# Five scheduler streams instead of three in a fused linear-attention and SwiGLU kernel

## The chip, the cores and the metric

The kernel runs on one core of one Trainium2 chip. The metric is the device time of one execution in microseconds (us), lower is better. "Time" is the median of several executions; "span" is the time from the first to the last instruction in the one execution that was profiled, and is about 1.7 us shorter than the time of the same execution. PE is the matmul engine (TensorE), PEld its loading of weights, DVE the vector engine, ACT the scalar engine, POOL the GpSimd engine, SP the engine that issues loads and stores.

## The reference, cut to what matters

`x` has 2048 rows of 640 numbers (16 tiles of 128 rows). The block is `x + A(norm(x)) + B(norm(x))`, where both branches read the same layer norm:

```python
xn = layernorm(x)
# A: attention with a learned feature map, 32 heads of 20
q, k, v = split(xn @ wqkv)
phi(u)  = concat(softmax(u @ w_phi), softmax(-u @ w_phi))      # per head
kv, z   = sum over all rows of phi(k)^T v,  sum of phi(k)      # needs every row
o       = phi(q) kv / (phi(q) . z)
A       = o @ wo
# B: SwiGLU
B       = (silu(xn @ w1) * (xn @ w3)) @ w2
```

Two facts of this shape matter. The sums over rows (`kv`, `z`) are a barrier: no output of attention can be made before the last key row has been normalised. The MLP (branch B) has no such barrier: each block of 512 rows needs only its own four normed tiles. The MLP is cut into 4 blocks of 12 chunks; a chunk is 10 matmuls of 128x512.

## The kernel before

A small scheduler in Python runs when the kernel is built. Streams (generators) yield steps; each step is a list of instructions with estimated costs. The scheduler always commits the step whose PE work could start first. Once committed, the order of instructions on each engine is fixed in the program, with a semaphore wait where an input comes from another engine. The timelines show the engines working through their lists in that order: in e2_coupled ACT stands 12.09 us for one instruction while a tanh that is ready stands behind it.

```python
def attention():                       # stream 1 of 3: (attention, mlps, outs)
    yield lambda: (loads(), consts())
    yield lambda: ln(0, 2); yield lambda: ln(2, 2)
    ... # fold w_phi into K's weights (fold_t, fold_mm), transpose x tiles 0-3
    for t in range(T):
        yield lambda t=t: kv_tile(t, banks("A", 4))     # K and V, exp, key normalise
        if t < 6:
            yield lambda t=t: ln(4 + 2 * t, 2)          # norms of two later tiles
        if t < 12:
            yield lambda t=t: xn_transpose(t + 4, banks("A", 1), "ACT" if t % 2 else "DVE")
        if t == 2:
            ... # fold_t for Q
            done["fold"] = True
    ... # q_proj(0), K/V sums; done["kv"] = True; then the query blocks

def ln(t0, n):      # DVE bn_stats, bn_aggr; POOL rstd = (var+eps)^-0.5; DVE (x-m)*rstd
    ...
def kv_tile(t, k):
    ... # 20 matmuls; ACT: exp(+), exp(-), copy of V; DVE: tensor_reduce, reciprocal
    ... # POOL: two multiplies of 128x640 ("key normalise")

def mlps():
    for b in range(NB):
        for fc in range(FC):
            while not done["fold"] or (b >= 2 and not done["kv"]):
                yield None                              # held
            yield lambda b=b, fc=fc: mlp(b, fc, banks("M", 2))
```

In the scheduler loop a step without PE work was committed at once (`at = -1.0`). `mlp` needs, for each chunk, one tanh on ACT and two products on DVE. `hT2`, the MLP's result for block 2, lay on the bytes of the keys (`ekt`), which is why block 2 was held until the K/V sums were done; `wqk_s` (weights of Q and K) lay on `hT1`.

The softmax here doesn't subtract the row's maximum and nothing guards it: scores larger than these inputs give would overflow.

Of the kernel before, what the change touches and what calls it, by code (L numbers as in the profile page):

```python
# [9 lines left out]
D = 640  # L10
# [18 lines left out]
class _Op:  # L29
    __slots__ = ("part", "eng", "emit", "reads", "writes", "cost", "dma", "deps", "start", "end",  # L30
                 "inc", "count", "sem", "clock", "idx")

    def __init__(self, eng, emit, reads, writes, cost, dma=False):
        self.eng, self.emit, self.reads, self.writes = eng, emit, reads, writes
        self.cost, self.dma = cost, dma
        self.part = False
        self.inc = False
        self.count = 0
        self.sem = None


class _Program:
# [52 lines left out]
    def op(self, eng, name, writes, reads, args, kw=None, cost=0.1):  # L95
# [4 lines left out]
        o = _Op(eng, lambda: m(*args, **kw), r, w, cost)  # L100
        o.part = eng == "POOL" and any(a.start_partition() != 0 for a in writes)
# [3 lines left out]
    def dma(self, eng, out, in_):  # L105
# [5 lines left out]
        o = _Op(eng, lambda: m(out, in_), self.regions(in_), self.regions(out), nbytes, True)  # L111
        self.pending.append(o)
# [36 lines left out]
    def ready(self, ops):  # L149
# [8 lines left out]
        return t  # L158

# [74 lines left out]
def bass_parallel_sum__linear_kernel_hedgehog__glu_gated_swiglu__prompt_kernel(  # L234
# [37 lines left out]
    bst = new("bst", [128, T, 2, 6], f32)  # L272
    mv = new("mv", [128, T, 2], f32)
    rstd = new("rstd", [128, T], f32)
# [14 lines left out]
    KVc = new("KVc", [128, 2, DC, D], bf, RX)  # L289
    ZG = new("ZG", [128, 2, DC, 64], bf, RX + 12800)  # L290
    wo_s = new("wo_s", [128, DC, D], bf, RX + 14080)
# [4 lines left out]
    EqT1 = new("EqT1", [128, 2, DC, 512], bf, RKV)  # L296
# [4 lines left out]
    wqk_s = new("wqk_s", [128, DC, 2 * D], bf, RH + 24576 - 12800)  # L301
# [3 lines left out]
    hT2 = new("hT2", [128, FC, 512], bf, RE)  # L305
    hT3 = new("hT3", [128, FC, 512], bf, RE + 12288)
    w2_s = new("w2_s", [128, FC, D], bf, RE + 24576)
# [8 lines left out]
    EqT0 = new("EqT0", [128, 2, DC, 512], bf, RW)  # L316
    EqT = [EqT0, EqT1]

    E_s = new("E_s", [128, 4, 128], f32, RW + 10240)
    den_s = new("den_s", [128, 4, 32], f32, RW + 12288)  # L320
# [47 lines left out]

    def memset(eng, o, v):
        P.op(eng, "memset", [o], [], (o, v), cost=0.15 + free(o) / 960)  # L370
# [14 lines left out]
    def loads():  # L385
        P.dma("SP", x_tok[:, 0:2, :], x_t[:, 0:2, :])
        P.dma("SP", x_tok[:, 2:4, :], x_t[:, 2:4, :])
        P.dma("SP", phi_s[:], phi_t)
        P.dma("SP", wqk_s[:, :, D:2 * D], wqkv_t[:, :, D:2 * D])
        P.dma("SP", wv[:], wqkv_t[:, :, 2 * D:3 * D])  # L390
        P.dma("SP", x_tok[:, 4:8, :], x_t[:, 4:8, :])
        P.dma("SP", x_tok[:, 8:12, :], x_t[:, 8:12, :])
        P.dma("SP", wqk_s[:, :, 0:D], wqkv_t[:, :, 0:D])
        for q in range(2):
            P.dma("SP", w1_s[:, :, 768 * q:768 * q + 768], w1_t[:, :, 768 * q:768 * q + 768])
            P.dma("SP", w3_s[:, :, 768 * q:768 * q + 768], w3_t[:, :, 768 * q:768 * q + 768])
            if q == 0:
                P.dma("SP", x_tok[:, 12:16, :], x_t[:, 12:16, :])
# [21 lines left out]
    def ln(t0, n):  # L420
        for t in range(t0, t0 + n):
            for q in range(2):
                i = x_tok[:, t, 320 * q:320 * q + 320]
                P.op("DVE", "bn_stats", [bst[:, t, q, :]], [i], (bst[:, t, q, :], i), cost=0.42)
            o, i = mv[:, t, :], bst[:, t, :, :].rearrange("p a b -> p (a b)")
            P.op("DVE", "bn_aggr", [o], [i], (o, i), cost=0.2)
        v, r = mv[:, t0:t0 + n, 1], rstd[:, t0:t0 + n]
        P.op("POOL", "tensor_scalar_add", [r], [v], (r, v, EPS), cost=0.3)
        tt("POOL", r, r, mhalf[:, 0:n], ALU.pow)
        for t in range(t0, t0 + n):  # L430
            o, m, s = x_tok[:, t, :], mv[:, t, 0:1], rstd[:, t:t + 1]
            P.op("DVE", "tensor_scalar", [o], [o, m, s], (o, o, m, s, ALU.subtract, ALU.mult),
                 cost=0.33)

    def xn_transpose(t, k, eng):
# [328 lines left out]
```

## Time and profile before

| | before |
|---|---|
| time, median of 3 runs | 354.18 us (353.96 to 354.21) |
| span | 352.9 us |
| PE busy | 313.8 us, 89% |
| first MLP matmul | 52.4 us |
| last K/V sum | 171.5 us |

The first two parts of the profile's page: the busy time of each engine, and tenths of busy time in 40 slices of 8.8 us.

```profile
PE 313.8 (89%) x2114; PEld 183.1 (52%) x2114; DVE 178.6 (51%) x299; ACT 117.7 (33%) x193; POOL 61.1 (17%) x68
PE   0582739968999999997999999999999999999996
PEclk9997878996999999999999999999999999999999
```

PE is the busiest engine, and its idle time is concentrated in the first nine slices. The clock that was granted to it is also lower there. The table of windows says how much (columns after the window's length: busy us of PE, PEld, DVE, ACT and POOL with the number of instructions, then granted clock, busy share of the DMA engines, GB/s):

```profile
0.00:18.00 18.00, 4.63 (x39) 3.99 (x39) 11.56 (x22) 5.77 (x9) 9.36 (x20) 1.00 0.92 302
18.00:80.00 62.00, 42.89 (x286) 26.11 (x286) 34.73 (x66) 24.69 (x38) 16.93 (x20) 0.88 0.17 59
80.00:172.00 92.00, 88.51 (x620) 53.78 (x621) 55.34 (x93) 40.42 (x64) 34.80 (x28) 0.97 0.03 10
172.00:350.00 178.00, 177.73 (x1170) 99.25 (x1170) 76.36 (x120) 46.78 (x82) 0.00 (x0) 1.00 0.13 41
```

After 172 us PE has almost no idle time. In the first 80 us it is busy 47.5 us, and no other engine is saturated either. So something makes them wait for one another. The timeline shows what (start, duration, engine, instruction, and in brackets idle time before it and whose end ended it):

```profile
26.43 1.49 DVE L100 TENSOR_REDUCE S_59<-ekt 128x64 f32<-128x1280 bf16 x1 [3.62 <-ACT ekt L100]
27.95 0.55 DVE L100 RECIPROCAL rS_60<-S_59 128x64 f32<-128x64 f32 x1
28.59 2.50 POOL L100 TENSOR_TENSOR ekt<-ekt,rS_60 128x640 bf16<-128x640 bf16 x2 [10.77 <-DVE rS_60 L100]
30.54 0.21 DVE L100 BATCH_NORM_AGGREGATE mv<-bst 128x2 f32<-128x12 f32 x1
31.05 0.22 POOL L100 TENSOR_SCALAR rstd<-mv 128x2 f32<-128x2 f32 x1
31.35 0.71 POOL L100 TENSOR_TENSOR rstd<-rstd,mhalf 128x2 f32<-128x2 f32 x1
32.09 0.80 DVE L100 TENSOR_SCALAR x_tok<-x_tok,mv,rstd 128x640 bf16<-128x640 bf16 x2 [1.34 <-POOL rstd L100]
32.60 0.72 PE L100 MATMUL PS<-ident,x_tok 128*128 128x128 bf16 x5 [6.18 <-DVE x_tok L100]
```

DVE sums the keys of one tile (reduce, reciprocal) and only then takes the statistics of the next x tiles; POOL normalises the keys (2.50 us) and only then computes `rstd` for those x tiles; DVE stands still for it, then applies the norm; PE has been idle for 6.18 us when the transpose of that tile may start. The chain of waits goes through this cycle five times before 80 us. (All lines of the kernel are L100 or L101, a helper; instructions are told apart by tile names.)

### The profile page before, as it was taken

Reading aid. Unit: us, or ns where it says so; the run is one execution under the profiler, and the core shown is the slowest. Engines: PE = TensorE matmul, PEld = TensorE weight load, DVE = VectorE, ACT = ScalarE, POOL = GpSimd, SP = SyncE. Lnnn points to the kernel's source line nnn. Section 1 sums busy time; section 2 is a strip of 40 time slices with the busy share of each in tenths; the row PEclk is TensorE's granted clock in tenths of the full one; section 3 lists DMA queues with packets and bytes.
Section 4 is the critical chain, followed back from the end, with each engine's and each line's share of the span. In section 5 each row is a group of like instructions: output and inputs, shape, how many; then the busy total and the mean of one; then the engine's idle time right before and its main releaser. Section 6 shows DMA issues by size and latency. Waiting matters only on the chain.

```text
span 352.9 us, 4956 instructions
## 1 busy us (share of the span) xinstructions
PE 313.8 (89%) x2114; PEld 183.1 (52%) x2114; DVE 178.6 (51%) x299; ACT 117.7 (33%) x193; POOL 61.1 (17%) x68
## 2 busy tenths in 40 slices
PE   0582739968999999997999999999999999999996
PEld 0461425534555555656744544544545577777774
DVE  4836563585886675632459349249289011111111
ACT  1440535532535435680352562472431300000000
POOL 2703330330323432494000000000000000000000
PEclk9997878996999999999999999999999999999999
DMA  7991000000000002000440000000000112222211
GB/s 233 368 371 54 0 0 3 0 1 2 1 0 2 0 2 93 2 1 2 126 154 0 2 0 2 0 2 1 0 3 0 39 37 76 74 76 74 76 56 37
DMA packets 14214, 17.38 MB, mean 49 GB/s; under 512 B 1392, under 2 KB 14192, under 8 KB 14192
## 3 DMA queue, kind: packets, MB, share of 16 engines
q1 hardware_dynamic: 14192, 17.07, 15.0%
q8 instruction: 16, 0.26, 0.3%
q14 instruction: 6, 0.05, 0.0%
HBM read 14.44 MB, written 2.62 MB: 48 GB/s over the span
## 4 chain that ended last, share of the span: by engine, by line
PE 77%; DVE 9%; POOL 9%; ACT 1%; issue 1%; DMA 1%; POOLq 0%
PE PS L100 77%; POOL ekt L100 5%; DVE S_59 L100 2%; DVE x_tok L100 2%; POOL rstd L100 2%; POOL KVc L100 2%; ACT ekt L100 1%; DVE bst L100 1%; DVE rS_60 L100 1%; DMA x_tok<-in_A_x_dram 1%; DVE BDc L100 1%; DVE t_66 L100 1%; DVE Wkp L100 0%; DVE xnT L100 0%; DVE mv L100 0%
## 5 line engine op out<-in xcount | busy, mean ns | idle before, releaser
L100 PE MATMUL PS<-xnT,w_s 128*128 128x512 bf16 x480 | 113.7, 388 | 4.2 <-DVE t_66 L100 4.2
L100 PEld LDWEIGHTS PS<-xnT,w_s 128*128 128x128 bf16 x480 | 45.8, 99 | 59.6 <-DVE t_66 L100 7.0
L100 POOL TENSOR_TENSOR ekt<-ekt,rS_60 128x640 bf16<-128x640 bf16 x32 | 39.9, 1269 | 92.5 <-DVE rS_60 L100 92.5
L100 DVE SCALAR_TENSOR_TENSOR t_66<-th,PS 128x512 bf16<-128x512 f32 x48 | 32.4, 675 | 32.2 <-ACT th L100 32.2
L100 ACT ACTIVATE th<-PS 128x512 f32<-128x512 f32 x48 | 28.7, 597 | 56.0 <-PE PS L100 55.8
L100 DVE TENSOR_TENSOR xres<-PS,xres 128x640 bf16<-128x640 f32 x16 | 13.2, 824 | 64.6 <-PE PS L100 64.6
L100 DVE TENSOR_REDUCE S_59<-ekt 128x64 f32<-128x1280 bf16 x16 | 23.7, 1484 | 25.5 <-ACT ekt L100 25.5
L100 ACT ACTIVATE ekt<-PS 128x640 bf16<-128x640 f32 x32 | 20.8, 701 | 34.7 <-PE PS L100 34.7
L100 PE MATMUL PS<-Wkp,xnT 128*128 128x320 bf16 x160 | 26.7, 319 | 1.8 <-ACT xnT L100 1.1
L100 PE MATMUL PS<-wv,xnT 128*128 128x320 bf16 x160 | 25.0, 305 | 0.0
L100 PE MATMUL PS<-wo_s,oT 128*128 128x320 bf16 x160 | 24.4, 300 | 0.0
L100 PE MATMUL PS<-xnT,Wqp 128*128 128x512 bf16 x100 | 22.3, 380 | 0.0
L100 PEld LDWEIGHTS PS<-Wkp,xnT 128*128 128x128 bf16 x160 | 16.1, 103 | 11.7 <-ACT xnT L100 1.3
L100 ACT ACTIVATE oT<-PS 128x512 bf16<-128x512 f32 x20 | 11.9, 597 | 24.4 <-PE PS L100 24.4
L100 PEld LDWEIGHTS PS<-wv,xnT 128*128 128x128 bf16 x160 | 16.0, 100 | 6.7
L100 PEld LDWEIGHTS PS<-wo_s,oT 128*128 128x128 bf16 x160 | 15.5, 98 | 6.4 <-issue 0.2
L100 PE MATMUL PS<-ident,wqk_s 128*128 128x128 bf16 x50 | 5.1, 283 | 14.4 <-DMA wqk_s<-in_A_wqkv_dram 8.7
L100 DVE BATCH_NORM_STATS2 bst<-x_tok 128x6 f32<-128x320 bf16 x32 | 15.0, 469 | 3.5 <-DMA x_tok<-in_A_x_dram 3.0
L100 PEld LDWEIGHTS PS<-xnT,Wqp 128*128 128x128 bf16 x100 | 9.5, 98 | 11.2 <-ACT ekt L100 0.4
L100 PE MATMUL PS<-ident,x_tok 128*128 128x128 bf16 x80 | 8.1, 248 | 7.5 <-DVE x_tok L100 7.5
L100 DVE TENSOR_SCALAR x_tok<-x_tok,mv,rstd 128x640 bf16<-128x640 bf16 x16 | 9.4, 627 | 10.3 <-POOL rstd L100 10.3
L100 PE MATMUL PS<-w_s,hT_76 128*128 128x320 bf16 x96 | 13.7, 299 | 0.0
(71 smaller groups left out, 347.7 us busy)
## 6 DMA issues: line engine op xcount, KB each, us to landing
w_s<-in_B_w_dram SPq DMA_DIRECT2D x4, 960.0 KB, 12.3
xres<-in_A_x_dram SPq DMA_DIRECT2D x16, 160.0 KB, 2.4
out_dram<-xres SPq DMA_DIRECT2D x16, 160.0 KB, 1.8
x_tok<-in_A_x_dram SPq DMA_DIRECT2D x3, 640.0 KB, 10.0
w_s<-in_B_w_dram SPq DMA_DIRECT2D x1, 1920.0 KB, 9.5
wqk_s<-in_A_wqkv_dram SPq DMA_DIRECT2D x2, 800.0 KB, 8.6
wv<-in_A_wqkv_dram SPq DMA_DIRECT2D x1, 800.0 KB, 8.1
wo_s<-in_A_wo_dram SPq DMA_DIRECT2D x1, 800.0 KB, 4.7
```

The source lines that it names most:

```text
L100: o = _Op(eng, lambda: m(*args, **kw), r, w, cost)
```

## The change

Its intent is to let each chain of dependent work run at its own pace, and to have MLP matmuls at hand wherever attention leaves PE idle. The core of the diff:

```diff
-    streams = [attention(), mlps(), outs()]
+    streams = [norms(), attention(), k_norms(), mlps(), outs()]
...
+    def norms():                        # runs ahead of attention by up to 4 tiles
+        ...
+        for t in range(4, T, 2):
+            while t > done["t"] + 4:
+                yield None
+            yield lambda t=t: ln_stats(t, 2)
+            if t > 4:
+                yield lambda t=t: ln_apply(t - 2)
+                yield lambda t=t: ln_apply(t - 1)
+    def k_norms():                      # reduce, reciprocal, POOL multiplies
+        for t in range(T):
+            while done["k"] <= t:
+                yield None
+            yield lambda t=t: k_norm(t)
...
     def attention():                    # V of tiles 0-3 first, then the K fold, then K
+        for t in range(4):
+            if t < 3:
+                yield from transposed(t + 1)
+            yield lambda t=t: v_tile(t, banks("A", 2))
...
-                while not done["fold"] or (b >= 2 and not done["kv"]):
+                while done["t"] < 4 * b + 4 or b == 2 and done["t"] < T or b == 3 and not done["kv"]:
...
-    hT2 = new("hT2", [128, FC, 512], bf, RE)          # on the keys
+    hT2 = new("hT2", [128, FC, 512], bf, RX)          # on x_tok
...
+    def ln_apply(t):                    # DVE, or ACT (Identity with scale and bias)
+        if t < 4 or P.free["DVE"] < P.free["ACT"]: ...
+    def evac(o, i):                     # a PSUM copy goes to whichever engine is free first
...
             else:
-                at = -1.0 (step without PE work: at once)
+                at = P.start_of(ops[0])
+                if i == 0 and at < P.free["PE"] + 2.0:
+                    at = -1.0
...
     loads: x0, x1, wv, x2-3, wk, phi, x4-7, w1/w3 third 1, x8-11, wq, third 2, x12-15, third 3
     (before: x0-1, x2-3, phi, wk, wv, x4-7, x8-11, wq, w1/w3 half 1, x12-15, half 2)
```

The number and shapes of the matmuls do not change (2114). Cut from the diff: `wqk_s` moves from `hT1` to the end of the keys' bytes, the product that builds `BDc` (`block_diag`) moves from DVE to POOL, and the late constants are made after the last norm.

More of the change, by code (lines that the diff above doesn't have):

```diff
@@ L29 @@
 class _Op:
-    __slots__ = ("part", "eng", "emit", "reads", "writes", "cost", "dma", "deps", "start", "end",
+    __slots__ = ("name", "part", "eng", "emit", "reads", "writes", "cost", "dma", "deps", "start", "end",
                  "inc", "count", "sem", "clock", "idx")
@@ L35, in __init__ @@
         self.cost, self.dma = cost, dma
+        self.name = ""
         self.part = False
@@ L100, in op @@
         o = _Op(eng, lambda: m(*args, **kw), r, w, cost)
+        o.name = name + ":" + ",".join(a.name for a in writes)
         o.part = eng == "POOL" and any(a.start_partition() != 0 for a in writes)
@@ L111, in dma @@
         o = _Op(eng, lambda: m(out, in_), self.regions(in_), self.regions(out), nbytes, True)
+        o.name = "dma:" + out.name
         self.pending.append(o)
@@ L158, in ready, with start_of @@
         return t
+    def start_of(self, o):
+        return max([self.free[o.eng]] + [d.end + 0.07 for d in self.find_deps(o)])
     def commit(self, ops):
@@ L271, in bass_parallel_sum__linear_kernel_hedgehog__glu_gated_swiglu__prompt_kernel @@
     BDc = new("BDc", [128, DC, 8 * DH], bf)
-    bst = new("bst", [128, T, 2, 6], f32)
-    mv = new("mv", [128, T, 2], f32)
-    rstd = new("rstd", [128, T], f32)
+    bst = new("bst", [128, T, 16], f32)
+    mv = new("mv", [128, T, 8], f32)
+    rstd = new("rstd", [128, T, 8], f32)
     mhalf = new("mhalf", [128, 4], f32)
@@ L288, in bass_parallel_sum__linear_kernel_hedgehog__glu_gated_swiglu__prompt_kernel @@
     x_tok = new("x_tok", [128, T, D], bf, RX)
-    KVc = new("KVc", [128, 2, DC, D], bf, RX)
-    ZG = new("ZG", [128, 2, DC, 64], bf, RX + 12800)
-    wo_s = new("wo_s", [128, DC, D], bf, RX + 14080)
+    hT2 = new("hT2", [128, FC, 512], bf, RX)
+    wo_s = new("wo_s", [128, DC, D], bf, RX + 12288)
+    ZG = new("ZG", [128, 2, DC, 64], bf, RX + 18688)
     RKV = region(12800)
@@ L295, in bass_parallel_sum__linear_kernel_hedgehog__glu_gated_swiglu__prompt_kernel @@
     wv = new("wv", [128, DC, D], bf, RKV + 6400)
-    EqT1 = new("EqT1", [128, 2, DC, 512], bf, RKV)
+    EqT0 = new("EqT0", [128, 2, DC, 512], bf, RKV)
     RH = region(24576)
@@ L300, in bass_parallel_sum__linear_kernel_hedgehog__glu_gated_swiglu__prompt_kernel @@
     hT1 = new("hT1", [128, FC, 512], bf, RH + 12288)
-    wqk_s = new("wqk_s", [128, DC, 2 * D], bf, RH + 24576 - 12800)
     RE = region(40960)
     ekt = new("ekt", [128, T, 2, D], bf, RE)
-    hT2 = new("hT2", [128, FC, 512], bf, RE)
-    hT3 = new("hT3", [128, FC, 512], bf, RE + 12288)
-    w2_s = new("w2_s", [128, FC, D], bf, RE + 24576)
+    hT3 = new("hT3", [128, FC, 512], bf, RE)
+    w2_s = new("w2_s", [128, FC, D], bf, RE + 12288)
+    EqT1 = new("EqT1", [128, 2, DC, 512], bf, RE + 27648)
+    E_s = new("E_s", [128, 4, 128], f32, RE + 37888)
+    den_s = new("den_s", [128, 4, 32], f32, RE + 39936)
+    wqk_s = new("wqk_s", [128, DC, 2 * D], bf, RE + 40960 - 12800)
     hT = [hT0, hT1, hT2, hT3]
@@ L315, in bass_parallel_sum__linear_kernel_hedgehog__glu_gated_swiglu__prompt_kernel @@
     wqkT = new("wqkT", [128, 2 * DC, D], bf, RW)
-    EqT0 = new("EqT0", [128, 2, DC, 512], bf, RW)
+    KVc = new("KVc", [128, 2, DC, D], bf, RW)
     EqT = [EqT0, EqT1]
-    E_s = new("E_s", [128, 4, 128], f32, RW + 10240)
-    den_s = new("den_s", [128, 4, 32], f32, RW + 12288)
     gT = new("gT", [64, 2, 512], bf, RKV + 10240)
@@ L367, in copy @@
             P.op(eng, "tensor_copy", [o], [i], (o, i), cost=0.14 + free(o) / 960 / fast)
+    def evac(o, i):
+        a = P.free["ACT"] + 0.17 + free(o) / 1200
+        d = P.free["DVE"] + 0.14 + free(o) / 960 / (2 if i.dtype == bf else 1)
+        copy("ACT" if a <= d else "DVE", o, i, 2 if i.dtype == bf else 1)
     def memset(eng, o, v):
@@ L385, in loads, with x, w13 @@
     def loads():
-        P.dma("SP", x_tok[:, 0:2, :], x_t[:, 0:2, :])
-        P.dma("SP", x_tok[:, 2:4, :], x_t[:, 2:4, :])
+        def x(a, b):
+            P.dma("SP", x_tok[:, a:b, :], x_t[:, a:b, :])
+        def w13(a, b):
+            P.dma("SP", w1_s[:, :, a:b], w1_t[:, :, a:b])
+            P.dma("SP", w3_s[:, :, a:b], w3_t[:, :, a:b])
+        x(0, 1)
+        x(1, 2)
+        P.dma("SP", wv[:], wqkv_t[:, :, 2 * D:3 * D])
+        x(2, 4)
+        P.dma("SP", wqk_s[:, :, D:2 * D], wqkv_t[:, :, D:2 * D])
         P.dma("SP", phi_s[:], phi_t)
-        P.dma("SP", wqk_s[:, :, D:2 * D], wqkv_t[:, :, D:2 * D])
-        P.dma("SP", wv[:], wqkv_t[:, :, 2 * D:3 * D])
-        P.dma("SP", x_tok[:, 4:8, :], x_t[:, 4:8, :])
-        P.dma("SP", x_tok[:, 8:12, :], x_t[:, 8:12, :])
+        x(4, 8)
+        w13(0, 512)
+        x(8, 12)
         P.dma("SP", wqk_s[:, :, 0:D], wqkv_t[:, :, 0:D])
-        for q in range(2):
-            P.dma("SP", w1_s[:, :, 768 * q:768 * q + 768], w1_t[:, :, 768 * q:768 * q + 768])
-            P.dma("SP", w3_s[:, :, 768 * q:768 * q + 768], w3_t[:, :, 768 * q:768 * q + 768])
-            if q == 0:
-                P.dma("SP", x_tok[:, 12:16, :], x_t[:, 12:16, :])
+        w13(512, 1024)
+        x(12, 16)
+        w13(1024, 1536)
     def consts():
@@ L417, in consts_late, with ln_stats, xn_transpose @@
             select(GT2[r:r + 32, :], DH, [[-1, D]], DH, ALU.is_gt, 0.0)
-    def ln(t0, n):
+    def ln_stats(t0, n):
         for t in range(t0, t0 + n):
             for q in range(2):
-                i = x_tok[:, t, 320 * q:320 * q + 320]
-                P.op("DVE", "bn_stats", [bst[:, t, q, :]], [i], (bst[:, t, q, :], i), cost=0.42)
-            o, i = mv[:, t, :], bst[:, t, :, :].rearrange("p a b -> p (a b)")
-            P.op("DVE", "bn_aggr", [o], [i], (o, i), cost=0.2)
-        v, r = mv[:, t0:t0 + n, 1], rstd[:, t0:t0 + n]
-        P.op("POOL", "tensor_scalar_add", [r], [v], (r, v, EPS), cost=0.3)
-        tt("POOL", r, r, mhalf[:, 0:n], ALU.pow)
-        for t in range(t0, t0 + n):
-            o, m, s = x_tok[:, t, :], mv[:, t, 0:1], rstd[:, t:t + 1]
-            P.op("DVE", "tensor_scalar", [o], [o, m, s], (o, o, m, s, ALU.subtract, ALU.mult),
-                 cost=0.33)
-    def xn_transpose(t, k, eng):
+                i, o = x_tok[:, t, 320 * q:320 * q + 320], bst[:, t, 6 * q:6 * q + 6]
+                P.op("DVE", "bn_stats", [o], [i], (o, i), cost=0.5)
+            o, i = mv[:, t, 0:2], bst[:, t, 0:12]
+            P.op("DVE", "bn_aggr", [o], [i], (o, i), cost=0.22)
+        m, v, r, z = mv[:, t0:t0 + n, 0], mv[:, t0:t0 + n, 1], rstd[:, t0:t0 + n, 0], rstd[:, t0:t0 + n, 1]
+        P.op("POOL", "tensor_scalar_add", [r], [v], (r, v, EPS), cost=0.25)
+        P.op("POOL", "tensor_tensor", [r], [r, mhalf[:, 0:n]], (r, r, mhalf[:, 0:n], ALU.pow),
+             cost=0.73)
+        if t0 >= 4:
+            P.op("POOL", "tensor_scalar_mul", [z], [m], (z, m, -1.0), cost=0.25)
+            P.op("POOL", "tensor_tensor", [z], [z, r], (z, z, r, ALU.mult), cost=0.25)
+    def ln_apply(t):
+        o, m, s, z = x_tok[:, t, :], mv[:, t, 0:1], rstd[:, t, 0:1], rstd[:, t, 1:2]
+        if t < 4 or P.free["DVE"] < P.free["ACT"]:
+            P.op("DVE", "tensor_scalar", [o], [o, m, s], (o, o, m, s, ALU.subtract, ALU.mult),
+                 cost=0.45)
+        else:
+            P.op("ACT", "activation", [o], [o, s, z], (o, o, ACT.Identity), dict(bias=z, scale=s),
+                 cost=0.9)
+    def xn_transpose(t, k):
         for dc in range(DC):
@@ L439, in xn_transpose @@
         src = PSb[:, k * 1024:k * 1024 + D].rearrange("p (c n) -> p c n", n=128)
-        copy(eng, xnT[:, :, t * 128:(t + 1) * 128], src, 2)
+        evac(xnT[:, :, t * 128:(t + 1) * 128], src)
     def block_diag():
@@ L446, in block_diag, with fold_t @@
             n = h1 - h0 + 1
-            tt("DVE", BDc[:, c, 0:n * DH].rearrange("p (h k) -> p h k", k=DH),
+            tt("POOL", BDc[:, c, 0:n * DH].rearrange("p (h k) -> p h k", k=DH),
                phi_s[:, c, :].unsqueeze(1).to_broadcast([128, n, DH]),
                GM[:, c, h0:h1 + 1].unsqueeze(2).to_broadcast([128, n, DH]), ALU.mult)
-    def fold_t(which, e, k, eng):
+    def fold_t(which, e, k):
         for dc in range(DC):
@@ L454, in fold_t, with fold_mm @@
                wqk_s[:, dc, which * D + 128 * e:which * D + 128 * e + 128])
-        copy(eng, wqkT[:, which * DC + e, :], PSb[:, k * 1024:k * 1024 + D], 2)
-    def fold_mm(which, dc, k, eng):
+        evac(wqkT[:, which * DC + e, :], PSb[:, k * 1024:k * 1024 + D])
+    def fold_mm(which, dc, k):
         first = [True, True]
@@ L468, in fold_mm, with proj, v_tile, k_tile @@
         dst = (Wqp, Wkp)[which]
-        copy(eng, dst[:, dc, :].rearrange("p (b c) -> p b c", c=320), bank2(k, 320))
-    def kv_tile(t, k):
-        for w, kk in ((Wkp, k), (wv, k + 2)):
-            for i in range(DC):
-                for q in range(2):
-                    mm(bank(kk + q, 320), xnT[:, i, t * 128:(t + 1) * 128],
-                       w[:, i, 320 * q:320 * q + 320], i == 0, i == DC - 1)
+        evac(dst[:, dc, :].rearrange("p (b c) -> p b c", c=320), bank2(k, 320))
+    def proj(t, w, k):
+        for i in range(DC):
+            for q in range(2):
+                mm(bank(k + q, 320), xnT[:, i, t * 128:(t + 1) * 128],
+                   w[:, i, 320 * q:320 * q + 320], i == 0, i == DC - 1)
+    def v_tile(t, k):
+        proj(t, wv, k)
+        pv = bank2(k, 320).rearrange("p b (h c) -> p b h c", c=DH)
+        act(v2[:, t, :].rearrange("p (b h c) -> p b h c", b=2, c=21)[:, :, :, 0:DH], pv, ACT.Copy)
+    def k_tile(t, k):
+        proj(t, Wkp, k)
         pk = bank2(k, 320)
@@ L481, in kv_tile, with k_norm @@
                 1.0 if sg == 0 else -1.0)
-        pv = bank2(k + 2, 320).rearrange("p b (h c) -> p b h c", c=DH)
-        act(v2[:, t, :].rearrange("p (b h c) -> p b h c", b=2, c=21)[:, :, :, 0:DH], pv, ACT.Copy)
+    def k_norm(t):
         s, r = S64[:, t % 3, :], rS64[:, t % 3, :]
@@ L557, in q_out @@
                n == 0, n == len(plan) - 1)
-        copy("ACT", oT[:, dc, b * 512:(b + 1) * 512], bank(k))
+        evac(oT[:, dc, b * 512:(b + 1) * 512], bank(k))
     nmlp = [0]
@@ L601, in banks @@
         return base + p % size
-    def attention():
-        yield lambda: (loads(), consts())
-        yield lambda: ln(0, 2)
-        yield lambda: ln(2, 2)
-        yield lambda: (block_diag(), consts_late())
+    done = dict.fromkeys(("ln", "t", "k", "n", "kv", "o", "h"), 0)
+    def norms():
+        yield lambda: (loads(), consts())
+        for t in range(4):
+            yield lambda t=t: ln_stats(t, 1)
+            if t:
+                yield lambda t=t: ln_apply(t - 1)
+                done["ln"] = t
+        yield lambda: ln_apply(3)
+        done["ln"] = 4
+        yield block_diag
+        for t in range(4, T, 2):
[4 more added lines that the diff above has]
+                yield lambda t=t: ln_apply(t - 2)
+                yield lambda t=t: ln_apply(t - 1)
+                done["ln"] = t
+        yield lambda: ln_apply(T - 2)
+        yield lambda: ln_apply(T - 1)
+        done["ln"] = T
+        yield consts_late
@@ new lines, in k_norms, with transposed @@
+    def k_norms():
[3 more added lines that the diff above has]
+            yield lambda t=t: k_norm(t)
+            done["n"] = t + 1
+    def transposed(t):
+        while done["ln"] <= t:
+            yield None
+        yield lambda: xn_transpose(t, banks("A", 1))
+        done["t"] = t + 1
+    def attention():
+        yield from transposed(0)
+        for t in range(4):
+            if t < 3:
+                yield from transposed(t + 1)
+            yield lambda t=t: v_tile(t, banks("A", 2))
@@ L608, in attention @@
         for e in range(DC):
-            yield lambda e=e: fold_t(1, e, banks("A", 1), "ACT")
-        for t in range(2):
-            yield lambda t=t: xn_transpose(t, banks("A", 1), "ACT")
+            yield lambda e=e: fold_t(1, e, banks("A", 1))
         for dc in range(DC):
-            yield lambda dc=dc: fold_mm(1, dc, banks("A", 2), "ACT" if dc % 2 else "DVE")
-        for t in range(2, 4):
-            yield lambda t=t: xn_transpose(t, banks("A", 1), "ACT")
+            yield lambda dc=dc: fold_mm(1, dc, banks("A", 2))
@@ L616, in attention @@
         for t in range(T):
-            yield lambda t=t: kv_tile(t, banks("A", 4))
-            if t < 6:
-                yield lambda t=t: ln(4 + 2 * t, 2)
-            if t < 12:
-                yield lambda t=t: xn_transpose(t + 4, banks("A", 1), "ACT" if t % 2 else "DVE")
-            if t == 2:
-                for e in range(DC):
-                    yield lambda e=e: fold_t(0, e, banks("A", 1), "ACT")
-                done["fold"] = True
-                for dc in range(DC):
-                    yield lambda dc=dc: fold_mm(0, dc, banks("A", 2), "ACT")
@@ L628, in attention @@
-            if t == 13:
-                yield kv_init
-                yield lambda: P.dma("SP", wo_s[:], A_wo.rearrange("(c p) d -> p c d", p=128))
+            yield lambda t=t: k_tile(t, banks("A", 2))
+            done["k"] = t + 1
+            if 2 <= t < 14:
+                yield from transposed(t + 2)
+            if t >= 4:
+                yield lambda t=t: v_tile(t, banks("A", 2))
+            if 4 <= t < 9:
+                yield lambda e=t - 4: fold_t(0, e, banks("A", 1))
+            if 9 <= t < 14:
+                yield lambda dc=t - 9: fold_mm(0, dc, banks("A", 2))
@@ L631, in attention @@
+        yield kv_init
+        yield lambda: P.dma("SP", wo_s[:], A_wo.rearrange("(c p) d -> p c d", p=128))
         for fc in range(DC):
             yield lambda fc=fc: q_proj(0, fc, banks("A", 1))
+        while done["n"] < T:
+            yield None
         for fc in range(DC):
@@ L635, in attention @@
                 yield lambda fc=fc, sg=sg: kv_sum(sg, fc, banks("A", 1))
-        done["kv"] = True
+        done["kv"] = 1
         yield lambda: P.dma("SP", w2_s[:], B_w2.rearrange("(c p) d -> p c d", p=128))
@@ L649, in attention @@
             done["o"] = b + 1
-    done = {"o": 0, "h": 0, "kv": False, "fold": False}
     def mlps():
@@ L665, in outs @@
             yield lambda t=t: out_tile(t, banks("M", 2))
-    streams = [attention(), mlps(), outs()]
-    heads = [None] * 3
-    alive = [True] * 3
+    streams = [norms(), attention(), k_norms(), mlps(), outs()]
+    n = len(streams)
+    heads, alive = [None] * n, [True] * n
     while any(alive):
         best = None
-        for i in range(3):
+        for i in range(n):
             if heads[i] is None and alive[i]:
@@ L676, in bass_parallel_sum__linear_kernel_hedgehog__glu_gated_swiglu__prompt_kernel @@
                     alive[i] = False
-                elif s is not None:
-                    save = dict(turn), nmlp[0], len(finish)
+                else:
                     heads[i] = s
@@ L681, in bass_parallel_sum__linear_kernel_hedgehog__glu_gated_swiglu__prompt_kernel @@
                 continue
-            save = dict(turn), nmlp[0]
-            nf = len(finish)
+            save = dict(turn), nmlp[0], len(finish)
             ops = P.step(heads[i])
-            after = dict(turn), nmlp[0], finish[nf:]
+            after = dict(turn), nmlp[0], finish[save[2]:]
             turn.update(save[0])
             nmlp[0] = save[1]
-            del finish[nf:]
-            if not any(o.eng == "PE" for o in ops):
-                at = -1.0
-            else:
-                at = max(P.ready(ops), P.free["PE"] + 0.15)
+            del finish[save[2]:]
+            if any(o.eng == "PE" for o in ops):
+                at = max(P.ready(ops), P.free["PE"] + 0.15)
+            else:
+                at = P.start_of(ops[0])
+                if i == 0 and at < P.free["PE"] + 2.0:
+                    at = -1.0
             if best is None or at < best[0]:
```

## The prediction

> **What bounds the kernel now.** TensorE. The page's busy table gives PE 89% of 352.9 us, DVE 51%, ACT 33%, POOL 17%; the chain of waits lies on PE for 77%. The table of windows shows regimes. From 172 to 350 us PE is busy 177.7 of 178 us at clock 1.00. From 0 to 80 us it is busy only 38 us, at clocks of 0.73 to 0.89 between 26 and 62 us. From 80 to 172 us it misses 3.5 us.
>
> In the first 80 us the chain is: x load, DVE statistics, POOL rstd (1.15 us with hops), then POOL key normalise (2.50 us a tile) holding the next rstd, DVE normalise, PE. The norm of tile t+4 stands behind reduce 1.49, reciprocal 0.55 and normalise 2.50 of tile t. The MLP, which could fill PE, is held until the Q fold has been transposed (first MLP matmul at 52.4 us). PE pauses of 6 us there also cost clock: the first ten MLP matmuls took 3.58 us against 2.32 later. [...]
>
> **What the change does.** Matmul work is unchanged (2114). It moves:
> - Norms run ahead of key normalise in their own stream.
> - V tiles need only x and wv, so PE starts real work at about 7.5 us.
> - MLP block 0 may start when 4 tiles are transposed and the first 512 columns of w1/w3 have landed: about 4.3 MB at the 0.37 MB/us of the DMA row, so about 15 us. K fold, K tiles and MLP then fill PE.
> - Added: POOL does two tiny ops per norm pair (0.23 us each) and the block diagonal; ACT takes some norms [...] and DVE some evictions. All off the chain if it is PE.
>
> **Sum.** From the dense windows: 512-column matmul 0.216 us, 320-column 0.135, small ones about 0.06; all 2114 about 300 us (estimate). Check: PE time after 80 us less its idle, 264 us, plus 37 us at the warm rate for what was done before, gives 301.
>
> Ramp: x0 lands at 3.2, xnT of tile 0 at 7.6, V tiles paced by norms (1.65 us of DVE a tile) until about 15.5 us, by when 6.5 us of warm work is done. Then 294 us remain, [...]plus the tail of 3.2 us, plus bubbles X. Span = 314 + X; time is 1.3 to 1.7 us above span. X: until the K/V sums DVE needs about 110 us of work (36 MLP x 1.36, 16 keys x 2.04, norms, copies) for 136 us of PE work, ACT about 75: so some bubbles where key normalise (2.04 us of DVE in one piece) delays the MLP products, whose two pairs of banks leave under 0.2 us of slack. Estimate X = 6.
>
> Prediction 321 us, range 314 to 332. Chances: faster 0.97, same 0.02, slower 0.01.
>
> **What would show it.** PE over 93% of the span; first MLP matmul near 15 us; PE nearly full at clock 1.0 in every window from 20 us; a shorter stretch from the K/V sums to the end, since MLP block 2 goes before it; POOL nearly gone from the chain.
>
> **What would make it wrong.** DVE the limit between 20 and 110 us (busy above 90%, PE waiting on DVE products); weights landing late[...]; PE order committed by wrong cost estimates, so that in-order engines wait on late norms; POOL's zeroing of the K/V tile (5.4 us) holding the sums with no MLP left to fill[...].

Cut was a term of the sum, 1.5 us for a slow start of PE: 15.5 + 294 + 1.5 + 3.2 came to the 314 us that the text gives; the terms that remain come to 313. "Warm" in it means the rate of the dense windows, at a granted clock of 1.00.

What the trace of the kernel before shows for the rest: after PE's waits of 6.18, 5.75 and 4.22 us the granted clock was 0.50 (windows 32.6 to 36, 51.4 to 54 and 80 to 84 us), and 1.00 again from 38, 56 and 86 us. A 160 KB load took 2.4 us to land (median of 16). Two tiles' statistics took 2.33 us of DVE and a pair of norms 0.80, which is 1.57 us a tile where the text has 1.65. A chunk took 2.16 us of PE, its tanh 0.60 us and its two products 0.68 and 0.69: the difference is 0.19 us, which agrees with the slack in the text.

## The result, and the profile after

| | before | after |
|---|---|---|
| time, median of 4 runs | 354.07 us (353.86 to 354.21) | 320.17 us (318.32 to 320.77) |
| ratio | | 0.9032, 95% interval 0.8999 to 0.9064 |
| span of the profiled run | 352.9 us | 316.6 us |
| first MLP matmul | 52.4 us | 18.8 us |
| last K/V sum | 171.5 us | 154.9 us |

A ratio is the mean time of one kernel's fast runs over that of the other's fast runs of the same rounds, so it is not quite the ratio of the medians. The same lines of the page, and the same windows, for the kernel after:

```profile
PE 300.7 (95%) x2088; PEld 178.8 (56%) x2114; DVE 177.6 (56%) x292; ACT 118.5 (37%) x195; POOL 67.2 (21%) x89
PE   0799999999999799999999999999999999999996
PEclk9999999999999999999999999999999999999999
```

```profile
0.00:18.00 18.00, 8.63 (x60) 5.86 (x61) 10.82 (x30) 6.59 (x10) 9.59 (x30) 1.00 0.95 300
18.00:80.00 62.00, 61.58 (x416) 36.40 (x423) 43.98 (x72) 41.13 (x65) 19.18 (x29) 1.00 0.19 60
80.00:172.00 92.00, 89.67 (x652) 53.41 (x662) 63.45 (x100) 41.77 (x70) 38.46 (x32) 1.00 0.12 37
```

From 18 to 80 us PE is now busy 61.6 of 62 us at a granted clock of 1.00, where it was busy 42.9 us at 0.88. (26 matmul records are missing from this trace, so small gaps in it are not real; the weight loads are complete, 2114.) The chain of waits, in its sums by engine, is nearly PE alone; first before, then after:

```profile
PE 77%; DVE 9%; POOL 9%; ACT 1%; issue 1%; DMA 1%; POOLq 0%
```

```profile
PE 94%; DMA 2%; ACT 1%; DVE 1%; issue 1%; SPq 0%
```

The gain of 36.3 us of span (the two profiled runs took 354.61 and 318.32 us; between the medians it is 33.9 us) can be placed on both sides of the barrier. The last K/V sum is ready 16.6 us sooner. And more MLP work is already done by then: the weight loads for w1 and w3 count 240 before the sums in the kernel before, which is 24 chunks, and 330, which is 33 chunks, after. A chunk takes 2.16 us of PE in the dense stretches, so 9 chunks are 19.4 us. The sum is 36.0 us. What follows the barrier was dense in both kernels; it is only shorter.

The ramp of the kernel after, on PE:

```profile
5.94 0.71 PE L101 MATMUL PS<-ident,x_tok 128*128 128x128 bf16 x5 [5.94 <-DVE x_tok L101]
9.05 0.71 PE L101 MATMUL PS<-ident,x_tok 128*128 128x128 bf16 x5 [2.40 <-DVE x_tok L101]
9.55 2.65 PE L101 MATMUL PS<-wv,xnT 128*128 128x320 bf16 x10
13.00 1.53 PE L101 MATMUL PS<-wv,xnT 128*128 128x320 bf16 x10 [0.52 <-ACT v_84 L101]
15.33 2.89 PE L101 MATMUL PS<-wv,xnT 128*128 128x320 bf16 x20 [0.52 <-ACT v_84 L101]
18.84 2.10 PE L101 MATMUL PS<-xnT,w_s 128*128 128x512 bf16 x9
```

The first V tile starts at 9.55 us, not at once when its weights and tile 0 are there, because the transpose of tile 1 stands ahead of it and waits for tile 1's norm; the chain shows why that norm is late: the load of x tiles 2 and 3 takes 5.21 us from issue to landing (at 7.39 us), DVE stands 1.53 us for it, and the statistics of tile 2 stand ahead of the norm on DVE. The first V tile is also slow: 2.65 us against 1.53 us for the next. (The granted-clock column does not show this: it reads 1.00 from 9 to 12 us and from 12 to 18 us. i2_all below shows the first V tile at 1.52 us after 4.05 us of other matmuls.)

### The profile page after: what moved, and what is told of

It is laid out like the page before. It is cut to its first block, busy times and chain, and to the rows that moved or that the text cites. A ratio compares the mean times of both kernels' runs of the same rounds, so it can differ in the third digit from the quotient of the medians.

```text
span 316.6 us, 4949 instructions
## 1 busy us (share of the span) xinstructions
PE 300.7 (95%) x2088; PEld 178.8 (56%) x2114; DVE 177.6 (56%) x292; ACT 118.5 (37%) x195; POOL 67.2 (21%) x89
## 4 chain that ended last, share of the span: by engine, by line
PE 94%; DMA 2%; ACT 1%; DVE 1%; issue 1%; SPq 0%
PE PS L101 94%; DMA x_tok<-in_A_x_dram 2%; ACT v_84 L101 1%; ACT ekt L101 0%; SPq L113 0%; DVE bst L101 0%; DVE xres L101 0%; DVE x_tok L101 0%; DVE KVc L101 0%; DVE mv L101 0%; DVE ZG L101 0%
## 5 line engine op out<-in xcount | busy, mean ns | idle before, releaser
L101 PE MATMUL PS<-xnT,w_s 128*128 128x512 bf16 x460 | 106.5, 379 | 1.1
L101 PE MATMUL PS<-Wkp,xnT 128*128 128x320 bf16 x160 | 24.2, 299 | 0.5 <-ACT v_84 L101 0.5
L101 ACT ACTIVATE oT<-PS 128x512 bf16<-128x512 f32 x14 | 8.4, 597 | 40.0 <-PE PS L101 40.0
L101 PE MATMUL PS<-xnT,Wqp 128*128 128x512 bf16 x96 | 21.4, 379 | 0.2
L101 PEld LDWEIGHTS PS<-Wkp,xnT 128*128 128x128 bf16 x160 | 15.5, 98 | 8.7 <-ACT v_84 L101 0.7
L101 ACT ACTIVATE v_84<-PS 128x640 bf16<-128x640 f32 x16 | 11.3, 707 | 15.5 <-PE PS L101 15.4
L101 PE MATMUL PS<-w_s,hT_75 128*128 128x320 bf16 x96 | 13.7, 299 | 0.0
L101 PE MATMUL PS<-w_s,hT_76 128*128 128x320 bf16 x96 | 13.7, 299 | 0.0
```

Of the source, the lines that this page charges most:

```text
L101: o = _Op(eng, lambda: m(*args, **kw), r, w, cost)
```

## The experiments

The total was forecast well, but the prediction did not say which part of the change carries it. My first theory (F) was: the gain is idle PE time filled by MLP work that the old gate held back. The rival (N): the gain is that norms no longer stand behind key normalise. A second rival (L): the new load order. All twelve kernels gave correct results. Sets that ran together share the runs of the kernel before, whose medians were 354.03 (first four), 354.74 (next four) and 354.51 us (last four). The changed kernel itself was not run again with them, so a difference of about 1 us between it and an experiment is not established; the ratios allow for the drift between sets.

| run | what it is | time us | ratio to before |
|---|---|---|---|
| after | the change | 320.17 | 0.9032 |
| e1_gate | MLP held until the Q fold | 337.49 | 0.9537 |
| e2_coupled | norms and key normalise coupled | 356.93 | 1.0073 |
| b1_gate | before, MLP block 0 let go early | 351.99 (3 fast runs) | 0.9925 |
| e3_loads | old load order | 330.39 | 0.9326 |
| e2b_dve | as e2_coupled, norms on DVE only | 336.91 | 0.9481 |
| e2d_first | as e2_coupled, norms first in the step | 340.40 | 0.9589 |
| e6_cap | e3_loads plus a cap on the lag | 321.09 | 0.9040 |
| e5_b2 | MLP block 2 held until the K/V sums | 330.36 | 0.9295 |
| e4_evac | all movable copies on ACT | 320.10 | 0.9023 |
| e8_both | e1_gate and e2b_dve at once | 343.15 | 0.9672 |
| i1_ramp | better ramp, with the cap | 315.24 | 0.8891 |
| i2_all | i1_ramp, throw-away matmuls first, split last tile | 313.74 | 0.8838 |

### e1_gate: undo the MLP's early start

```diff
-                while done["t"] < 4 * b + 4 or ...:
+                while not done["fold"] or done["t"] < 4 * b + 4 or ...:
... (and the flag "fold", set once the Q weights have been transposed)
```

> Changed kernel, but every MLP block is held until the Q fold has been transposed, as before the change. Theory F (the gain is mostly idle PE time filled by MLP work that the gate no longer holds back): 332 to 340 us, first MLP matmul near 55 us, PE busy well under 80% between 20 and 55 us. Rival N (the gain is mostly that norms no longer stand behind key normalise on POOL and DVE): at most 324 us.

Measured: 337.49 us, so taking the early start away costs about 17 of the 34 us; F's number held. PE is busy 48.0 us of the 62 between 18 and 80 us (after: 61.6). The undo goes further than meant: the changed kernel transposes the Q weights later, so the first MLP matmul comes at 64.0 us, not near 55 as expected nor at 52.4 as before the change. PE is idle 4.2 of the 11.6 us between 52.4 and 64.0 us, so some of the 17 us belong to this. Attention alone, although decoupled, does not fill PE in this run: it waits for exp and V copies on ACT to free PSUM banks (7.4 us for exp, 3.4 us for V in the list of waits).

### e2_coupled: undo the split of the streams

```diff
-            yield lambda t=t: k_tile(t, banks("A", 2))
+            yield lambda t=t: (k_tile(t, banks("A", 2)), k_norm(t), ln_pair(4 + 2 * t))
... (the loop over tiles 4 to 15 in norms() goes; ln_pair does its work)
-    streams = [norms(), attention(), k_norms(), mlps(), outs()]
+    streams = [norms(), attention(), mlps(), outs()]
```

> Changed kernel, but key normalise and the norms of the next two tiles are issued with each K tile in one stream, as before the change; MLP gate, loads, V order, overlays and evictions stay changed. Theory F: 322 to 330 us, because MLP work covers most of the slower norms. Rival N: 334 us or more, with POOL and DVE norms back on the chain.

Measured: 356.93 us, no faster than the kernel before (ratio 1.0073, interval 1.0050 to 1.0096). F's number fell by a wide margin and N's held: with norms coupled in this way, all the MLP work in reach does not help. The timeline shows the mechanism:

```profile
47.29 0.72 POOL L101 TENSOR_TENSOR rstd<-rstd,mhalf 128x2 f32<-128x2 f32 x1
48.64 1.73 ACT L101 ACTIVATE x_tok<-x_tok,rstd 128x640 bf16<-128x640 bf16 x2 [12.09 <-POOL rstd L101]
50.28 0.57 ACT L101 ACTIVATE th<-PS 128x512 f32<-128x512 f32 x1
50.89 0.69 DVE L101 SCALAR_TENSOR_TENSOR t<-th,PS 128x512 bf16<-128x512 f32 x1 [4.32 <-ACT th L101]
51.63 4.45 PE L101 MATMUL PS<-xnT,w_s 128*128 128x512 bf16 x10 [9.07 <-DVE t L101]
```

ACT's next instruction in order is the norm of a tile whose `rstd` comes late; it stands for 12.09 us. The tanh of an MLP chunk that was ready stands behind it, the MLP's product behind that, and PE, which could run MLP matmuls if a PSUM bank were free, is idle for 9.07 us. Here an MLP chunk is filler only while ACT and DVE are free to empty its banks.

But this undo mixed two things. The kernel before applied norms on DVE only; here the changed kernel's choice to put some on ACT met the old coupling. e2b_dve separates them.

### b1_gate: the MLP gate alone, in the kernel before

```diff
... (and done["t"] = 4 once four tiles are transposed)
-                while not done["fold"] or (b >= 2 and not done["kv"]):
+                while (done["t"] < 4 if b == 0 and fc < 11 else not done["fold"]) or (b >= 2 and not done["kv"]):
```

> Kernel before, with one change alone: MLP block 0 may start when four tiles are transposed (its last chunk still waits for the Q fold, whose weights share its bytes). Theory F: 335 to 343 us, first MLP matmul near 23 us instead of 52 us. Rival N: 348 us or more, since the norms still hold the K tiles and DVE.

Measured: 351.99 us, the median of three fast runs that lie far apart (349.19 to 353.41; the fourth, 356.26 us, was slow). The ratio is 0.9925 (0.9870 to 0.9980), almost nothing; F's number fell and N's held. Its windows show a gain that is given back:

```profile
18.00:80.00 62.00, 53.62 (x344) 31.26 (x351) 40.12 (x71) 28.30 (x44) 13.57 (x16) 0.90 0.18 61
80.00:172.00 92.00, 80.41 (x584) 50.67 (x589) 49.80 (x88) 36.69 (x59) 38.22 (x32) 0.93 0.04 10
```

PE is busy 10.7 us more than before between 18 and 80 us, and 8.1 us less between 80 and 172 us. The loss has two parts. One is a single wait of 4.24 us while there were still MLP chunks to run: the product of an MLP chunk stands on DVE behind a norm that waits for `rstd`, and PE behind the product.

```profile
84.36 0.80 DVE L100 TENSOR_SCALAR x_tok<-x_tok,mv,rstd 128x640 bf16<-128x640 bf16 x2 [1.33 <-POOL rstd L100]
85.08 0.68 DVE L100 SCALAR_TENSOR_TENSOR t<-th,PS 128x512 bf16<-128x512 f32 x1
85.82 4.45 PE L100 MATMUL PS<-xnT,w_s 128*128 128x512 bf16 x10 [4.24 <-DVE t L100]
```

The other lies after 122 us. The MLP has 24 chunks to give before the barrier in either case, because block 2 is still locked. Spent early, they are missing later: the last weight load of the last chunk before the sums starts at 121.8 us (143.1 us in the kernel before), and K and V tiles run alone from there with gaps (PE busy 42.9 of the 50 us to 172, 47.3 in the kernel before).

### e3_loads: the old load order in the changed kernel

> Changed kernel with the load order of before (V still computed ahead of K). Theory F: 319 to 324 us: V starts about 2 us later because its weights land later, MLP about 1 us later. Rival L (the reordered loads are a large part of the gain): 326 us or more.

(The edit is the order of the loads only, as listed under the change.) Measured: 330.39 us, 10 us lost: L's number. But the trace shows two separate places. V's first tile starts at 11.43 us instead of 9.55, the first MLP chunk at 25.9 instead of 18.8 us. More is lost at the barrier:

```profile
154.96 0.69 DVE L101 SCALAR_TENSOR_TENSOR t<-th,PS 128x512 bf16<-128x512 f32 x1 [0.75 <-ACT th L101]
156.29 1.48 DVE L101 TENSOR_REDUCE S<-ekt 128x64 f32<-128x1280 bf16 x1
158.44 4.95 POOL L101 TENSOR_TENSOR ekt<-ekt,rS 128x640 bf16<-128x640 bf16 x4 [15.39 <-DVE rS L101]
159.76 0.30 PE L101 MATMUL PS<-v,ekt 128*128 128x147 bf16 x1 [3.49 <-POOL ekt L101]
162.22 9.96 PE L101 MATMUL PS<-v,ekt 128*128 128x147 bf16 x121 [2.15 <-POOL ekt L101]
```

The key normalise of the last two tiles was committed after all remaining MLP products of block 2. DVE did it when no MLP chunk was left, and PE waited 5.6 us for POOL. Why it got there is visible in the scheduler: a step without PE work is now ordered by when DVE is free, an MLP step by when PE is free, and while DVE's list is longer than PE's, the MLP step always comes first. Key normalise starves until the MLP runs out. In both kernels the query projection leaves DVE a gap from 131 to 137 us, in which it does three tiles' keys. In the kernel after three were left by then, here five.

### e6_cap: the old load order, with the starvation taken away

```diff
+                if i == 2 and done["k"] - done["n"] > 2:     # key normalise over two tiles behind
+                    at = -1.0
```

> The kernel of e3_loads (load order of before) with one rule added: key normalise may not fall more than two tiles behind the K tiles, so that its last two tiles no longer stand behind all remaining MLP products. Theory S (half of the 10 us that e3_loads lost is this starvation before the K/V sums, the other half the later start): 323 to 327 us, and the 5.6 us of PE waiting for POOL gone. Rival (the load order alone costs it): 329 us or more.

Measured: 321.09 us, better than theory S expected. So nearly all of the 10 us of e3_loads goes when the starvation goes; the old load order together with the cap cannot be told from the change (ratio 0.9040, 0.9005 to 0.9074, against 0.9032). (The cap on the changed kernel alone was not run, so the later start by itself may cost more than this shows.) PE's wait for POOL is gone from the list of waits, and PE is busy 113.3 of the 114 us from 26 to 140 us. Rival L falls: the load order mattered because it changed what the scheduler committed, not much by itself.

### e2b_dve: coupled, norms on DVE only

```diff
... (all of e2_coupled, and)
-        if t < 4 or P.free["DVE"] < P.free["ACT"]:
+        if True:
```

> The coupled kernel of run e2_coupled, with every norm applied on DVE, so that ACT never stands waiting for POOL's rstd. If ACT's wait in order (12 us in one piece in e2_coupled) is what the coupling costs: 343 to 350 us. If it is the coupling itself, on whatever engine: 354 us or more.

Measured: 336.91 us, lower than either expectation. About 20 us of the 37 us by which e2_coupled was slower than the change was the mix of the old coupling with norms on ACT, a mix that neither the kernel before nor the kernel after has. The coupling with all norms on DVE costs about 17 us against the change; norms apart but all on DVE were not run, so what the coupling costs by itself is not shown. DVE still stands about 2 us for `rstd` before each pair of norms, and PE is busy 51.0 of the 62 us between 18 and 80 us (after: 61.6), but ACT keeps emptying banks.

### e2d_first: coupled, norms before key normalise

```diff
-  (k_tile(t, banks("A", 2)), k_norm(t), ln_pair(4 + 2 * t))
+  (k_tile(t, banks("A", 2)), ln_pair(4 + 2 * t), k_norm(t))
```

> The coupled kernel of e2_coupled with one exchange: in each step the norms of the next two tiles are issued before this tile's key normalise, not after it. Theory N1 (what costs is that POOL's rstd stands behind reduce, reciprocal and 2.5 us of normalise, and the in-order engines behind it): 326 to 340 us. Theory N2 (one step for both makes norms too late wherever they stand): 345 us or more.

Measured: 340.40 us, just above N1's range and below N2's. One exchange in the order won back 16.5 us of e2_coupled, so the place of the norm matters, but not all of it: PE still waits 9.2 us for MLP products and 10.4 us for norms in this run. It keeps some norms on ACT, so it is not clean. How the 17 us of the coupling divide between the place in the step and the lateness of the step stays open.

### e5_b2: MLP block 2 locked until the barrier

```diff
-   b == 2 and done["t"] < T or b == 3 and not done["kv"]:
+   b >= 2 and not done["kv"]:
```

> Changed kernel with MLP block 2 held until the K/V sums are done, as before the change, where the tile it writes lay on the keys; everything else as changed. If the new overlay matters as filler: 325 to 332 us, with a hole of PE before the K/V sums. If it is only a convenience: at most 322 us.

Measured: 330.36 us, 10 us lost, as the overlay theory said. The kernel runs out of MLP chunks (240 weight loads before the sums) and PE has holes; in the second window POOL is busy nearly all the time:

```profile
100.00:120.00 20.00, 16.76 (x126) 10.85 (x126) 17.43 (x21) 9.63 (x16) 11.23 (x10) 1.00 0.13 41
120.00:140.00 20.00, 14.56 (x122) 9.62 (x122) 8.05 (x14) 9.41 (x16) 19.93 (x15) 0.98 0.00 1
```

The change of overlay, moving `hT2` from the keys to the bytes of `x`, looks like housekeeping in the diff. It unlocks nine chunks of filler.

### e4_evac: all movable copies on ACT

```diff
-        copy("ACT" if a <= d else "DVE", o, i, ...)
+        copy("ACT", o, i)
```

> Changed kernel with every one of the movable PSUM copies on ACT, as mostly before. If PE stays the limit: 319 to 324 us, since ACT is at most 76% busy in any window of the changed kernel's first 100 us. If the free choice of engine carries part of the gain: 327 us or more, with PE waiting for ACT copies.

Measured: 320.10 us, no difference. The free choice of engine for PSUM copies is not part of the gain in this kernel.

### e8_both: the two undos at once

> Changed kernel with two undos at once: MLP held until the Q fold (e1_gate, about 17 us alone) and norms and key normalise coupled, applied on DVE (e2b_dve, about 17 us alone). If each covers its own idle time the losses add: 351 to 358 us. If they are two ways into the same idle time of PE: 337 to 346 us.

Measured: 343.15 us. Alone, each undo cost 17 us; together they cost 23 us, not 34. Theory F and theory N are therefore not rivals: early MLP work and decoupled norms are two ways to close largely the same idle time in the first 100 us, and of these four kernels only the one with both has PE full there (61.6 of 62 us between 18 and 80 us; 48.0, 51.0 and 44.6 in the other three). (The hold on the MLP goes too far here as in e1_gate: the first MLP matmul comes at 66.0 us.) With both undone the kernel is still 11 us faster than the one before. That is left to the rest of the change, whose parts were not told apart in this state; V ahead of K, and the moves of `BDc` and of the late constants, were never undone.

| changed kernel | norms apart | norms coupled (DVE) |
|---|---|---|
| MLP early | 320.17 | 336.91 |
| MLP held until the Q fold | 337.49 | 343.15 |

### i1_ramp and i2_all: a version that beats both

i1_ramp loads x tiles 2 and 3 before V's weights, the first third of w1/w3 before x tiles 4 to 7, gives the first four V tiles the MLP's idle PSUM banks, and has the cap.

```diff
-        x(0, 1); x(1, 2); wv; x(2, 4); wk; phi; x(4, 8); w13(0, 512); ...
+        x(0, 1); x(1, 2); x(2, 4); wv; wk; phi; w13(0, 512); x(4, 8); ...
-            yield lambda t=t: v_tile(t, banks("A", 2))          # tiles 0 to 3
+            yield lambda t=t: v_tile(t, banks("M", 2))
```

> Changed kernel, meant to be better: x tiles 2 and 3 loaded before V's weights, first MLP weights before x tiles 4 to 7, the first four V tiles in the MLP's idle PSUM banks, and the cap on key normalise of e6_cap. If the ramp (PE idle about 9 us before 18 us) is set by the load of x tiles 2 and 3, by norms waiting for it, and by V's copies: 314 to 318 us, first MLP matmul near 15 us instead of 18.8. If something else sets it: 319 us or more.

i2_all adds 44 throw-away matmuls on the identity matrix at the start, and sums and stores the last output tile in two halves:

```diff
-        yield lambda: (loads(), consts())
+        yield lambda: (loads(), consts(), [mm(bank(7, 128), ident[:], ident[:], True, True) for _ in range(44)])
...
+        if t == T - 1:
+            for q in range(2):      # columns 0-319, then 320-639
+                ... # 17 matmuls, DVE add of this half, store of this half
```

> i1_ramp with 44 throw-away matmuls on the identity from about 2 us on, [...]and the last output tile summed and stored in two halves. Expected 1 to 2.5 us below i1_ramp: V tile 0 takes 1.5 us instead of 2.65, the time from last matmul to end 2.7 us instead of 3.1. [...]

(The alternative: equal to i1_ramp within 0.5 us if the slow tile costs nothing on the chain.)

Measured: i1_ramp 315.24 us (0.8891, interval 0.8854 to 0.8928), i2_all 313.74 us (0.8838, interval 0.8800 to 0.8875). PE's first V tile and first MLP chunk, i1_ramp then i2_all:

```profile
8.08 2.83 PE L101 MATMUL PS<-wv,xnT 128*128 128x320 bf16 x10
15.48 1.56 PE L101 MATMUL PS<-ident,wqk_s 128*128 128x128 bf16 x25
16.88 2.32 PE L101 MATMUL PS<-xnT,w_s 128*128 128x512 bf16 x10
```

```profile
1.60 4.05 PE L101 MATMUL PS<-ident 128*128 128x128 bf16 x44 [1.60 <-POOL ident L101]
8.48 1.52 PE L101 MATMUL PS<-wv,xnT 128*128 128x320 bf16 x10 [0.25 <-DMA wv<-in_A_wqkv_dram]
15.86 2.32 PE L101 MATMUL PS<-xnT,w_s 128*128 128x512 bf16 x10
```

The first MLP chunk starts 2.0 us sooner in i1_ramp than in the kernel after, less than I expected, and the time fell by 4.9 us, so the cap and the other edits took part; they were not told apart. In i2_all, with the throw-away matmuls in front (4.05 us of PE), the first V tile goes from 2.83 to 1.52 us (the granted clock reads 1.00 from 0 to 18 us in both runs), the first MLP chunk moves 1.0 us forward, and the time from the last sum to the end shrinks by 0.5 us (from 3.1 to 2.6). That is the whole difference of 1.5 us between the two spans (312.6 and 311.1 us). The intervals of the two ratios overlap, so that i2_all is faster than i1_ramp rests on the traces and on the runs of these rounds, of which all six of i2_all are faster than five of the six of i1_ramp; that either is faster than both kernels does not need the traces.

## Why the prediction was right

The time was forecast as 321 us, and 320.17 us was measured.

- **PE is the limit, and its work is constant.** Right. The estimate of 300 us for all matmuls agrees: from 18.06 us, when V and its transposes are done, to 313.5 us, when PE ends, lie 295.4 us; less the 2.1 us in which the waits list shows PE idle, 293.3 us of work, where the sum had 294.
- **A reading in it was wrong.** It says PE was busy 38 us in the first 80 us of the kernel before. The windows add up to 47.5 us. The sum did not use that number, only the 37 us estimated for the same work at the rate of the dense windows.
- **The chain in the first 80 us.** Named rightly, but not its weights: the text puts POOL's 2.50 us of key normalise in front of the next `rstd`, where the trace before shows it beside DVE's statistics, ending 0.3 us after them. e2d_first, which lets the norms go first on both engines, won back 16.5 us of the 37 that e2_coupled had lost.
- **Ramp.** Too short. The sum let V tiles start at 7.5 us and end at 15.5; they started at 9.55 and ended at about 18.1 us. It paced them by DVE's work on norms (1.65 us a tile) and mentioned no order: tile 1's norm stood behind the statistics of tile 2, whose load landed at 7.39 us, and V copies on ACT held PE twice for 0.52 us. The first MLP chunk came at 18.8 us, not 15.
- **Bubbles X.** Too long: 6 us estimated, 2.1 us measured after 18 us. I feared key normalise on DVE would delay MLP products. DVE was indeed busy 8.3 of 9 us between 71 and 80 us, but PE stayed full, since the committed order alternates K, V and MLP chunks, and the two kinds use different PSUM banks.
- **The errors cancelled in part.** The ramp was 2.6 us longer (1.1 us if the cut term of 1.5 us is counted in, since the measured ramp contains the slow first V tile; that the tile would cost 1.5 us was not shown), the bubbles 3.9 us shorter. The forecast span was 320 us; the profiled one, of the fastest of the four timed runs, was 316.6 us. That the median time came within 1 us of the forecast is partly luck.
- **What would show it.** PE 95% (forecast over 93%), nearly full windows from 20 us at clock 1.00 (the worst, 100 to 120 us, has 18.3 of 20), a shorter stretch after the K/V sums, and POOL gone from the chain: right. Only the first MLP matmul was not near 15 us.
- **What it did not say.** It named the norms and the MLP gate as moves, without weights. The experiments give them: each about 17 us alone as an undo (with the reservations above), overlapping; the overlay of block 2 about 10 us; the old load order nothing that can be told from noise when the cap comes with it; choice of copy engine nothing. My own first theory after the result, that the MLP gate was the larger cause, fell in b1_gate and e2_coupled. It also did not see how thin the result is: e3_loads shows that a small edit elsewhere tips the scheduler's order and costs 10 us at the barrier.

## What to carry to other kernels

In these runs filler work filled the bottleneck engine only when three things held at once: its inputs were ready, the in-order engines that must empty its results were not standing behind a wait of some other chain (ACT stood 12.09 us in e2_coupled), and enough of it was left when the hole came (in e5_b2, with no chunk left, PE was busy 14.56 us of the 20 from 120 us on). Check the stretch up to the next barrier as a whole, since filler spent early can be missing later. Avoid that an in-order engine's next instruction is one whose input comes late from another engine; put such chains in streams of their own and let them run ahead. In a list scheduler, compare steps by the same clock or bound the lag of each stream, or work that is off the limit today may starve until it is the limit, as in e3_loads.

## What else the traces show

- The gap of 6.18 us in the kernel before was an instruction order on DVE and POOL (statistics behind reduce and reciprocal, `rstd` behind 2.50 us of key normalise); the chain of waits shows no buffer there.
- A norm on DVE that met a POOL memset of 2.36 to 2.37 us took 2.97 to 2.99 us in each of the seven traces read where the two met (before, after, b1_gate, e3_loads, e5_b2, i1_ramp, i2_all). In the kernel after, one norm on DVE, 0.41 us as a median, took 2.97 us while POOL ran two memsets of 2.37 and 0.95 us. In e2_coupled, where the same memset met no norm, no norm on DVE took over 0.53 us in the timelines of its first 58 us. The kernel before had the same in its ramp, where it lay on the chain: two norms took 3.77 us, against 0.80 us elsewhere. So about 3 us of the gain (an estimate, 3.77 less 0.80) may come from the constants' later place, which the prediction did not name; no run takes it away alone, so that the memset is the cause is not shown. The norm and the memset it met, in the kernel before and in the kernel after:

```profile
11.64 2.36 POOL L100 MEMSET v_82<- 128x512 bf16 x1
11.73 3.77 DVE L100 TENSOR_SCALAR x_tok<-x_tok,mv,rstd 128x640 bf16<-128x640 bf16 x2 [1.14 <-POOL rstd L100]
76.38 2.37 POOL L101 MEMSET v_84<- 128x512 bf16 x1
76.49 2.97 DVE L101 TENSOR_SCALAR x_tok<-x_tok,mv,rstd 128x640 bf16<-128x640 bf16 x1 [0.46 <-POOL rstd L101]
```

- One norm on ACT took 0.916 us as a median in the kernel after, where ACT took 0.70 us for other instructions of 128x640 in the kernel before.
- POOL's two tiny instructions for `rstd` (128x2 elements) take 0.22 and 0.71 us in the kernel before, about 1.1 us with the hops, in the middle of a chain that DVE and PE wait for.
